# Chunked attention inside an expert block: one visit of TensorE per group, the second head's state in the other half of the partitions, and one load and the stores at other places in their queues

## The chip, the cores and the metric

The kernel runs on one core of a Trainium2 chip. The metric is the device time in microseconds, the median of three runs. TensorE (PE), VectorE (DVE), ScalarE (ACT) and GpSimd (POOL) compute; SyncE (SP) issues all transfers between the chip's memory and the on-chip memory.

## The reference, cut to what matters

```
# B, H, S, D = 4, 8, 768, 48
for t in range(S):
    kt, vt, rt = (k[:, :, t], v[:, :, t], r[:, :, t])
    cur = np.einsum('bhd,bhe->bhde', u[None] * kt, vt)
    y[:, :, t] = np.einsum('bhd,bhde->bhe', rt, state + cur)
    state = w[None, :, :, None] * state + np.einsum('bhd,bhe->bhde', kt, vt)
x = y.transpose(0, 2, 1, 3).reshape(B * S, H * D)          # 3072 x 384
gate = 1.0 / (1.0 + np.exp(-(x @ w_gate)))                 # 384 x 1536
val = x @ w_val
return gate * val @ w_out                                  # 1536 x 384
```

A recurrent attention with a 48 x 48 state per batch and head feeds a gated two-layer block.

## The kernel before, in words

**Attention.** The 768 steps are cut into 12 chunks of 64, and each chunk has two groups of heads, so there are 24 groups (`GROUPS`), numbered n. Per group the kernel computes scores of keys against decayed queries within the chunk (`scores`), keeps their lower triangle (`keep`, VectorE), multiplies them by the values (`apply`), adds what earlier chunks left (`from_state`, queries times state), and makes the state's update (`outer`). These are 16 small float32 matmuls each, 48 or 64 wide, which work in the four 64 x 64 quarters of the array. `decay_state` (ScalarE) scales the state; `add_state` (VectorE) adds the update. The output of a group lies in two PSUM banks (`yb`): `x_high` (ScalarE) rounds it into the block's input, `x_low` (VectorE) keeps the rest, and `fills` moves a few rows by transfers.

**What a group needs.** `load_channels` fetches `chan`, `load_tokens` fetches `toks` and, from group 8 on, `dec<-in_rt`. `queries` (GpSimd) writes `dec` from `chan`, `keys` (VectorE) changes `chan`, `own_tokens` (GpSimd) multiplies `dec`'s second half in two steps, `token_keys` (GpSimd) changes `toks`, and `diagonal` (VectorE) reduces what `own_tokens` made and writes the scores' diagonal. `prepare(n)` is these five.

**The block.** Tokens come in 6 tiles of 512 columns (two chunks), and each tile has 12 slices f of 128 hidden channels; an item is one tile and slice. `up` is 18 matmuls into two banks, `sigmoid` (ScalarE), `product` (VectorE), `h_high` (ScalarE) and `h_low` (GpSimd) make the hidden values in two parts, and `down` is 9 matmuls into three accumulators `acc`. `down` of an item runs behind the next item's `up`. It takes its passes in this order: six matmuls on `h_high`, three on `h_low`. After a tile's last slice, `store` copies each accumulator out, half by ScalarE and half by VectorE, through `wf` tiles of which there are two, and issues the transfer.

**PSUM.** Eight banks: two for the scores (`sc`), three for the accumulators, and a ring of three that `up`'s two banks and a group's two output banks take in turn.

**Order.** Every engine works through its own list in the order in which the program was written; nothing reorders it. The opening is written out step by step in the table `START` (groups 0 to 7, tile 0, all weights): a letter names a step and a number its group or item (`Z` scores, `K` keep, `I` apply, `O` outer, `d` decay, `s` add, `h` and `l` the input's two parts, `U`, `g`, `m`, `H`, `q`, `D` the block, `L`, `X` loads, `R`, `k`, `b`, `T`, `i` the five of `prepare`). Then the loop over the items of tiles 1 to 5 runs, and slices 0, 3, 6 and 9 (`SLOTS`) of tiles 1 to 4 each carry one group, 8 to 23. In a slot before, TensorE visits the group twice: `from_state` and `scores` behind `up`, then the previous item's `down`, then `apply` and `outer`. In the opening `apply` runs `from_state` itself and has TensorE drain in between.

Of the kernel before, what the change touches and what calls it, by code (L numbers as in the profile page):

```python
# [10 lines left out]
F32 = mybir.dt.float32  # L11
# [4 lines left out]
ALU = mybir.AluOpType  # L16
# [4 lines left out]
P = 128  # L21
C = 64
# [22 lines left out]
s.0 I.1 k.2 O.1 R.2 F.0 X.3 s.1 h.1 A.3 Z.2 o0.0 W.3 X.4 l.1 L.4 K.2 W.7 T.2 U.0 R.3 g.0 k.3 I.2  # L45
O.2 c.3 W.4 Z.3 j.2 h.2 d.2 l.2 R.4 m.0 s.2 H.0 F.2 K.3 A.4 j.3 U.1 L.5 g.1 X.5 I.3 w.2 h.3 qv.0
d.3 T.4 T.3 w.3 D.0 k.4 O.3 l.3 R.5 s.3 m.1 Z.4 A.5 U.2 o.2 c.4 g.2 K.4 H.1 I.4 d.4 k.5 O.4 h.4
j.4 X.6 qv.1 Z.5 W.6 w.4 m.2 s.4 H.2 D.1 l.4 o.3 U.3 L.6 L.7 c.5 qv.2 D.2 W.11 g.3 K.5 F.4 o.4 A.6
m.3 j.5 H.3 Tv.5 U.4 g.4 R.6 qv.3 w.5 m.4 W.9 ov.5 F.1 I.5 O.5 H.4 D.3 d.5 h.5 k.6 Z.6 s.5 l.5 A.7
U.5 c.6 F.3 q.4 D.4 g.5 k.7 X.7 j.6 F.5 c.7 m.5 H.5 U.6 T.6 j.7 w.7 K.6 q.5 W.10 D.5 o.7 g.6 w.6  # L50
Rv.7 m.6 H.6 q.6 U.7 c.9 g.7 Z.7 ov.6 I.6 O.6 h.6 d.6 j.9 m.7 D.6 W.8 l.6 s.6 c.8 H.7 w.9 U.8 j.8
q.7 D.7 T.7 g.8 w.8 m.8 o.9 H.8 ov.8 q.8 U.9 g.9 D.8 K.7 U.10 c.10 m.9 c.11 H.9 j.10 g.10 I.7 q.9
m.10 O.7 H.10 h.7 l.7 d.7 w.10 D.9 q.10 s.7 ub L.8 X.8 U.11 D.10 g.11 j.11 m.11 o.10 U.12 F.6 H.11
w.11 g.12 ov.11 q.11 R.8 k.8 b.8 T.8 i.8 m.12 H.12 D.11 U.13 qv.12 g.13 m.13 H.13 qv.13 D.12 F.7
"""


# [1 line left out]
def rwkv_then_moe(ctx: ExitStack, tc: tile.TileContext, wd, ub, ch, tk, rt, wt, rk0, vn0, wd0, out):  # L59
# [20 lines left out]
    def one_bank():  # L80
        return ring.tile([P, 512], F32, name="ring")
# [232 lines left out]
    def into_y(n, half, bank, m, cs, lhsT, rhs, stop):  # L314
# [4 lines left out]
            start=first, stop=stop, skip_group_check=True,  # L319
        )  # L320

    def from_state(n):
        c, g = GROUPS[n]
        for p, p2 in PP:
            for s in range(2):
                for be in range(2):
                    row, m = slice(64 * be, 64 * be + D), D if s else 64
                    at = (4 * (2 * g + p) + 2 * s + p2) * D
                    i = (4 * p + 2 * s + p2) * C
                    into_y(  # L330
                        n, s, be, m, slice((2 * p + p2) * C, (2 * p + p2 + 1) * C),
                        state[row, at : at + m], dec[n][row, 0, i : i + C], False,
                    )


# [1 line left out]
    def scores(n):  # L337
        t, r, k = dec[n], chan[n][:, 0], chan[n][:, 1]
        sc = ga[n] = two_banks()
        if n >= FIRST:  # L340
# [12 lines left out]

    def keep(n):
        sc, t = ga.pop(n), score[n % 2]
        for m, at in ((0, 0), (1, 256))[: 2 if n < FIRST else 1]:
            nc.vector.copy_predicated(  # L357
                t.rearrange("q (b m i) -> q b m i", b=2, m=4),
                masks[:, m].bitcast(I32).unsqueeze(1).unsqueeze(1).broadcast_to([P, 2, 4, C]),
                sc[:, :, at : at + 256].rearrange("q b (m i) -> q b m i", m=4),  # L360
            )

    def apply(n):
        c, g = GROUPS[n]
        v, t = toks[n][:, 1], score[n % 2]
        if n < FIRST:
            yb[n] = one_bank(), one_bank()
            if c:
                from_state(n)
                nc.tensor.drain()  # L370
        for p, p2 in PP:
            for s in range(2):
                for gm in range(2):
                    be, row = gm ^ s, slice(64 * gm, 64 * gm + 64)
                    m, at = D if s else 64, (4 * p + 2 * be + p2) * D
                    i = (4 * be + 2 * p + p2) * C
                    into_y(
                        n, s, be, m, slice((2 * p + p2) * C, (2 * p + p2 + 1) * C),
                        v[row, at : at + m], t[row, i : i + C], True,
                    )  # L380
# [10 lines left out]
                        v[row, at : at + D], True,  # L391
                    )

    def states(n):
        g = GROUPS[n][1]
        st = state[0:112, 8 * g * D : 8 * (g + 1) * D]
        return g, st.rearrange("q (p s x) -> q p s x", p=2, s=2)

    def decay_state(n):
        g, st = states(n)  # L400
        for p in range(2):
            for s in range(2):
                nc.scalar.activation(  # L403
                    st[:, p, s], st[:, p, s], AF.Copy,
                    scale=pw[0:112, 4 * g + 2 * p + s, 64:65],
                )

    def add_state(n):
        g, st = states(n)
        for s in range(2):  # L410
            y = yb[n][s][0:112, 256 : 256 + 4 * D].rearrange("q (p x) -> q p x", p=2)
            if GROUPS[n][0]:
                nc.vector.tensor_tensor(st[:, :, s], st[:, :, s], y, ALU.add)  # L413
            else:
# [160 lines left out]
    def idle_matmuls(k):  # L575
# [40 lines left out]
    def load(n):  # L616
        if n < len(GROUPS):
            load_channels(n)
            load_tokens(n)
# [214 lines left out]
```

## Time and profile before

| | us |
|---|---|
| median of 3 runs | 565.53 |
| lowest and highest run | 565.0, 570.23 |
| span of the profiled execution | 564.3 |
| `up` of tile 1's first slice begins | 136.85 |
| first of a slot's matmuls to the next slot's, f = 0 of tile 2 | 22.13 |
| the same, f = 3 of tile 2 | 21.31 |

The span runs from the first to the last instruction of the profiled execution; the run's time also holds the launch and the end around it. The page gives no other time of the profiled execution. Busy time counts an instruction from start to modelled end, so a busy TensorE is not TensorE at its peak.

### The profile page before, as it was taken

The numbers are of one execution on the slowest core, as the hardware profiler recorded it, in microseconds if no ns is written. First come the engines' busy times: TensorE is split into PE (matmuls) and PEld (weight loads), VectorE is DVE, ScalarE is ACT, GpSimd is POOL, SyncE is SP. The second block draws the span as 40 slices with busy tenths as digits, with TensorE's granted clock in tenths as the row PEclk, the third lists the DMA queues.
The fourth block names the chain that finished last, engine by engine and source line by source line (L and its number), as shares of the span: only waits on it lengthen the run. The fifth ranks groups of instructions, "written<-read, shape, count | busy, mean of one in ns | idle before, by whom it ended". The sixth has DMA issues, their size and how long they took to land. (4 is left out here: it accounts for less than half of the span.)

```text
span 564.3 us, 11903 instructions
## 1 busy us (share of the span) xinstructions
PE 526.4 (93%) x5204; PEld 425.6 (75%) x5204; DVE 222.0 (39%) x348; ACT 170.5 (30%) x358; POOL 209.1 (37%) x165
## 2 busy tenths in 40 slices
PE   1595899999999999999999999999999999999995
PEld 1484778877778778778778788788788777888884
DVE  7798799964422322413313413313313311100101
ACT  4466446541322221322222322222312221212121
POOL 3534233843442533424424324524414411221121
PEclk9999799999999999999999999999999999999999
DMA  8699711030500203410203320113230001100001
GB/s 328 262 358 372 303 31 23 2 101 1 200 19 2 91 1 100 157 62 1 61 32 100 116 95 9 40 51 100 80 125 15 8 5 20 57 0 2 0 1 59
DMA packets 15721, 47.83 MB, mean 85 GB/s; under 512 B 2384, under 2 KB 5200, under 8 KB 14256
## 3 DMA queue, kind: packets, MB, share of 16 engines
q1 hardware_dynamic: 15664, 47.01, 23.7%
q8 instruction: 43, 0.70, 0.5%
q14 instruction: 14, 0.11, 0.1%
HBM read 39.92 MB, written 4.72 MB: 79 GB/s over the span
## 5 line engine op out<-in xcount | busy, mean ns | idle before, releaser
L477 PE MATMUL ring<-xt,wx 128*128 128x512 f32 (+1 forms) x1332 | 320.0, 393 | 4.0 <-DVE state L413 2.6
L477 PEld LDWEIGHTS ring<-xt,wx 128*128 128x128 f32 x1332 | 246.8, 191 | 61.1 <-PE ring L477 4.2
L499 POOL TENSOR_TENSOR h<-sg,h 128x512 fp32r<-128x512 f32 x68 | 93.0, 1367 | 309.9 <-ACT h L495 309.9
L515 PE MATMUL acc<-h,wx 128*128 128x512 f32 (+1 forms) x666 | 164.5, 391 | 1.0 <-DVE h L499 0.7
L490 DVE TENSOR_TENSOR sg<-ring,sg 128x512 f32<-128x512 f32 (+1 forms) x74 | 50.0, 676 | 255.1 <-PE ring L477 251.7
L515 PEld LDWEIGHTS acc<-h,wx 128*128 128x128 f32 x666 | 122.2, 190 | 28.3 <-DVE h L499 0.9
L486 ACT ACTIVATE sg<-ring 128x512 f32<-128x512 f32 (+1 forms) x74 | 43.4, 586 | 158.8 <-PE ring L477 158.3
L495 ACT CAST h<-sg 128x512 fp32r<-128x512 f32 (+1 forms) x74 | 45.0, 609 | 152.0 <-DVE sg L490 152.0
L278 POOL TENSOR_TENSOR dec<-chan,tabk 128x512 f32<-128x512 f32 x22 | 30.6, 1390 | 11.9 <-DMA chan<-in_ch 11.9
L440 DVE TENSOR_TENSOR xt<-ring,xt 112x256 fp32r<-112x256 f32 (+1 forms) x52 | 19.9, 418 | 38.0 <-ACT xt L436 37.1
L246 POOL TENSOR_TENSOR wx<-wf,wx 128x1152 fp32r<-128x1152 f32 (+1 forms) x9 | 24.9, 2768 | 23.6 <-ACT wx L243 23.6
L349 PE MATMUL sc<-dec,chan 48*64 48x64 f32 x768 | 17.3, 231 | 12.2 <-DVE chan L284 10.2
L436 ACT CAST xt<-ring 112x256 fp32r<-112x256 f32 (+1 forms) x52 | 17.1, 374 | 33.7 <-PE ring L317 32.6
L357 DVE COPY_PREDICATED score<-masks,sc 128x512 f32<-128x512 int32 x32 | 24.0, 749 | 6.1 <-PE sc L349 5.8
L288 POOL TENSOR_TENSOR toks<-toks,tabn 128x384 f32<-128x384 f32 x19 | 26.2, 1380 | 0.0
L317 PEld LDWEIGHTS ring<-score,toks 64*48 64x48 f32 (+1 forms) x768 | 14.1, 133 | 14.3 <-issue 12.1
L349 PEld LDWEIGHTS sc<-dec,chan 48*64 48x64 f32 x768 | 14.8, 145 | 13.2 <-DVE chan L284 9.4
L317 PE MATMUL ring<-score,toks 64*48 64x64 f32 (+1 forms) x768 | 17.5, 230 | 7.5 <-DVE score L357 6.5
L403 ACT ACTIVATE state<-state,pw 112x96 f32<-112x96 f32 x80 | 23.4, 365 | 0.3 <-PE ring L317 0.2
L237 DVE SCALAR_TENSOR_TENSOR wf<-wr,wf 128x1152 int32<-128x1152 int32 (+1 forms) x13 | 22.5, 1734 | 0.5
L284 DVE TENSOR_TENSOR chan<-chan,tabk 128x512 f32<-128x512 f32 x24 | 20.1, 838 | 2.9 <-ACT dec L272 2.9
L317 PEld LDWEIGHTS ring<-dec,state 48*48 48x48 f32 (+1 forms) x704 | 12.2, 127 | 8.8 <-issue 6.3
(56 smaller groups left out, 238.9 us busy)
## 6 DMA issues: line engine op xcount, KB each, us to landing
wr<-in_wt SPq DMA_DIRECT2D x11, 1152.0 KB, 10.3
chan<-in_ch SPq DMA_DIRECT2D x24, 512.0 KB, 4.3
toks<-in_tk SPq DMA_DIRECT2D x24, 400.0 KB, 4.5
out_y<-wf SPq DMA_DIRECT2D x17, 256.0 KB, 2.2
dec<-in_rt SPq DMA_DIRECT2D x16, 192.0 KB, 4.1
xt<-xt SPq DMA_DIRECT2D x30, 64.0 KB, 2.3
wr<-in_wt SPq DMA_DIRECT2D x2, 576.0 KB, 5.4
xt<-xt SPq DMA_DIRECT2D x12, 32.0 KB, 3.1
```

The lines of the kernel that those rows point to most:

```text
L246: eng.tensor_tensor(wlo[f][:, c], w32[f][:, c], whi[f][:, c], ALU.subtract)
L278: eng.tensor_tensor(v4(t[:, 0]), v4(chan[n][:, 0]), bc2(table_of(n)[:, :, ::-1]), ALU.mult)
L288: eng.tensor_tensor(v4(k), v4(k), bc2(tabn[:, 4 * g : 4 * g + 4]), ALU.mult)
L317: nc.tensor.matmul(yb[n][bank][64 * half : 64 * half + m, cs], lhsT, rhs, start=first, stop=stop, skip_group_check=True,)
L349: nc.tensor.matmul(sc[64 * gm : 64 * gm + 64, be, o : o + C], kk[row, cs : cs + C], rr[row, cs : cs + C], start=True, stop=True,)
L357: nc.vector.copy_predicated(t.rearrange("q (b m i) -> q b m i", b=2, m=4), masks[:, m].bitcast(I32).unsqueeze(1).unsqueeze(1).broadcast_to ...
L477: nc.tensor.matmul(o[:, self.cols], w[a][:, g * DM + kt * P : g * DM + (kt + 1) * P], self.x[:, kt, b, self.cols], start=(k == 0), stop=(k ...
L486: nc.scalar.activation(sg[:, c], self.pair[f][0][:, c], AF.Sigmoid)
L490: nc.vector.tensor_tensor(sg[:, c], self.pair.pop(f)[1][:, c], sg[:, c], ALU.mult)
L495: nc.scalar.copy(out=h[:, 0, c], in_=sg[:, c])
L499: eng.tensor_tensor(h[:, 1, c], self.sg.pop(f)[:, c], h[:, 0, c], ALU.subtract)
L515: nc.tensor.matmul(self.acc[d][:, self.cols], w[a][:, 2 * DM + d * P : 2 * DM + (d + 1) * P], h[:, b, self.cols], start=(f == 0 and k == 0 ...
```

## The change

- In the loop TensorE visits a group once: `outputs` (its two banks and `from_state`), `scores` of the group after, `apply`, `outer`, all behind `up` and ahead of the previous item's `down`. `Z.8` and `K.8` and all of group 9's preparation move into `START`; `prepare` works two groups ahead, `load` three.
- The state of the second of two heads (s = 1) lies in the other 64 partitions than before. `turn_queries` makes two ScalarE copies of these heads' queries into the other half, and `add_state` adds in three pieces instead of two. Each output region is then written by one half of the rows in `from_state` and `apply` alike, and the drain is left out.
- The third load of a group, `dec<-in_rt`, becomes `load_own`, which `prepare(n)` issues (`Y` in `START`) instead of `load_tokens`.
- `finish` (with the stores of a finished tile) comes behind `x_high`, `x_low`, `add_state` and `keep` in the order of ScalarE and VectorE.

```
 START = """
...
+j.10 g.10 I.7 q.9 m.10 O.7 H.10 h.7 l.7 d.7 w.10 D.9 q.10 s.7 ub L.8 X.8 Y.8 L.9 X.9 Y.9 U.11 D.10
...
+R.9 t.9 qv.12 k.9 g.13 m.13 H.13 Z.8 K.8 qv.13 b.9 T.9 i.9 D.12 F.7
...
-        if n >= FIRST:
-            nc.sync.dma_start(out=dec_of(n)[:, 1, 0 : 8 * D], in_=rt[c, g])
+    def load_own(n):
+        c, g = GROUPS[n]
+        nc.sync.dma_start(out=dec_of(n)[:, 1, 0 : 8 * D], in_=rt[c, g])
...
+    def turn_queries(n):
+        for lo, to in ((0, 64), (64, 0)):
+            src = dec[n][lo : lo + 64, 0].rearrange("q (p s x) -> q p s x", p=2, s=2)
+            nc.scalar.copy(out=turned(n)[to : to + 64], in_=src[:, :, 1])
...
+    def outputs(n):
+        yb[n] = one_bank(), one_bank()
+        if GROUPS[n][0]:
+            from_state(n)
...
     def from_state(n):
...
-                    row, m = slice(64 * be, 64 * be + D), D if s else 64
+                    lo = 64 * (be ^ s)
+                    row, m = slice(lo, lo + D), D if s else 64
...
     def apply(n):
...
         if n < FIRST:
-            yb[n] = one_bank(), one_bank()
-            if c:
-                from_state(n)
-                nc.tensor.drain()
+            outputs(n)
...
     def add_state(n):
-        g, st = states(n)
-        for s in range(2):
-            y = yb[n][s][0:112, 256 : 256 + 4 * D].rearrange("q (p x) -> q p x", p=2)
+        for s, to, lo, rows in ((0, 0, 0, 112), (1, 0, 64, D), (1, 64, 0, D)):
...
     def prepare(n):
         if n < len(GROUPS):
+            load_own(n)
             queries(n)
+            turn_queries(n)
             keys(n)
...
         m.up(f)
+        attend = f in SLOTS and n < 4 * (ti + 2) and n < len(GROUPS)
+        goes_on = attend and GROUPS[n][0] < NC - 1
+        if attend:
+            outputs(n)
+            if n + 1 < len(GROUPS):
+                scores(n + 1)
+            apply(n)
+            if goes_on:
+                outer(n)
         m.gate(f)
...
+        if goes_on:
+            decay_state(n)
         if attend:
-            scores(n)
-            if GROUPS[n][0] < NC - 1:
-                decay_state(n)
-            keep(n)
+            x_high(n)
+            x_low(n)
+            if goes_on:
+                add_state(n)
+            if n + 1 < len(GROUPS):
+                keep(n + 1)
         finish(i - 1)
         if attend:
-            apply(n)
-            if GROUPS[n][0] < NC - 1:
-                outer(n)
-            x_high(n)
-            x_low(n)
-            if GROUPS[n][0] < NC - 1:
-                add_state(n)
-            prepare(n + 1)
+            prepare(n + 2)
             fills(n)
-            load(n + 2)
+            load(n + 3)
             n += 1
```

TensorE's rows in the slot of f = 0 in tile 1, from the end of `from_state` to the start of `apply`, before (`ring` is a bank of the ring, `sc` the scores):

```order
L317 MATMUL ring<-dec,state 64x64 x2
L317 MATMUL ring<-dec,state 48x64 x2
L349 MATMUL sc<-dec,chan 64x64 x16
L515 MATMUL acc_429<-h,wx 128x512 x3
L515 MATMUL acc_430<-h,wx 128x512 x3
L515 MATMUL acc_431<-h,wx 128x512 x3
L317 MATMUL ring<-score_98,toks 64x64 x2
```

and after:

```order
L330 MATMUL ring<-dec,state 64x64 x2
L330 MATMUL ring<-chan,state 48x64 x2
L366 MATMUL sc<-dec,chan 64x64 x16
L330 MATMUL ring<-score_97,toks 64x64 x2
L330 MATMUL ring<-score_97,toks 48x64 x2
```

The `down` between the two visits has gone from here; it stands behind `outer`.

SyncE's list at the same slot, from the last loads issued ahead of it, before (`out_y` is the store, `in_rt` the third load of a group):

```order
L101 DMA chan<-in_ch 128x1024
L106 DMA toks<-in_tk 128x800
L108 DMA dec<-in_rt 128x384
L529 DMA out_y<-wf 128x512 x3
L101 DMA chan<-in_ch 128x1024
```

and after:

```order
L102 DMA chan<-in_ch 128x1024
L107 DMA toks<-in_tk 128x800
L545 DMA out_y<-wf 128x512 x3
L111 DMA dec<-in_rt 128x384
L102 DMA chan<-in_ch 128x1024
```

The third load of the group that `prepare` works on stood ahead of the three stores and now stands behind them.

VectorE's list in the slot of f = 0 in tile 2, before:

```order
L357 COPY_PREDICATED score_98<-masks,sc 128x512
L528 COPY wf<-acc_1629 128x256
L528 COPY wf<-acc_1630 128x256
L528 COPY wf<-acc_1631 128x256
L440 TENSOR_TENSOR xt<-ring,xt 112x2x128 x2
L413 TENSOR_TENSOR state<-state,ring 112x2x96 x2
L284 TENSOR_TENSOR chan<-chan,tabk 128x512
L299 TENSOR_REDUCE bonus_108<-dec 128x2x2x2
L304 TENSOR_TENSOR score_99<-masks,bonus_108 128x512
L490 TENSOR_TENSOR sg<-ring,sg 128x512 x3
```

and after:

```order
L456 TENSOR_TENSOR xt<-ring,xt 112x2x128 x2
L429 TENSOR_TENSOR state<-state,ring 112x2x96
L429 TENSOR_TENSOR state<-state,ring 48x2x96 x2
L374 COPY_PREDICATED score_98<-masks,sc 128x512
L544 COPY wf<-acc_1675 128x256
L544 COPY wf<-acc_1676 128x256
L544 COPY wf<-acc_1677 128x256
L297 TENSOR_TENSOR chan<-chan,tabk 128x512
L312 TENSOR_REDUCE bonus_106<-dec 128x2x2x2
L317 TENSOR_TENSOR score_97<-masks,bonus_106 128x512
L506 TENSOR_TENSOR sg<-ring,sg 128x512 x3
```

The three copies of the stores stood ahead of `x_low` (`xt<-ring`) and the state's add, and now stand behind them and behind `keep`; the reduction of `diagonal` (`bonus<-dec`) still stands ahead of the next item's `product` (`sg<-ring`).

## Rows read from the trace of the kernel before

**Rows 1.** The profile's page, its first part: busy time of TensorE and its weight loads, share of the span, and instructions, then the other engines.

```profile
PE 526.4 (93%) x5204; PEld 425.6 (75%) x5204; DVE 222.0 (39%) x348; ACT 170.5 (30%) x358; POOL 209.1 (37%) x165
```

**Rows 2.** The wait view of the whole span: who waited for what, us in total, times, the longest.

```profile
PE ring L477 <- DVE state L413: 2.6, 4, 0.8
```

**Rows 3.** Timeline of TensorE, tile 1 and the two undisturbed slots of tile 2 (f = 3 and 6 begin at 249.61 and 270.92). Columns: start us, us to the end of the last of the group, engine, line, operation, out<-in, count, and in brackets the idle time before it and what ended it.

```profile
184.53 0.68 PE L317 MATMUL ring<-dec,state 48*64 48x64 f32 x32
185.02 0.65 PE L349 MATMUL sc<-dec,chan 48*64 48x64 f32 x32
185.60 2.32 PE L515 MATMUL acc<-h,wx 128*128 128x512 f32 x9
187.85 0.68 PE L317 MATMUL ring<-score,toks 64*64 64x64 f32 x32
188.35 0.64 PE L317 MATMUL ring<-toks 64*48 64x48 f32 x32
188.92 4.44 PE L477 MATMUL ring<-xt,wx 128*128 128x512 f32 x18
193.20 2.25 PE L515 MATMUL acc<-h,wx 128*128 128x512 f32 x9
195.29 4.34 PE L477 MATMUL ring<-xt,wx 128*128 128x512 f32 x18
199.46 2.25 PE L515 MATMUL acc<-h,wx 128*128 128x512 f32 x9
...
249.61 0.68 PE L317 MATMUL ring<-dec,state 48*64 48x64 f32 x32
...
270.92 0.68 PE L317 MATMUL ring<-dec,state 48*64 48x64 f32 x32
```

**Rows 4.** Timeline of all engines, same columns: the slot of f = 0 in tile 2, where tile 1's accumulators are stored (SPq is SyncE's queue).

```profile
227.48 0.68 PE L317 MATMUL ring<-dec,state 48*64 48x64 f32 x32
...
228.71 0.76 DVE L357 COPY_PREDICATED score<-masks,sc 128x512 f32<-128x512 int32 x1 [0.36 <-PE sc L349]
228.91 1.17 ACT L403 ACTIVATE state<-state,pw 112x96 f32<-112x96 f32 x4
...
230.82 3.32 SPq L529 DMA_DIRECT2D out_y<-wf  x3
...
231.58 1.02 POOL L294 TENSOR_TENSOR dec<-dec,toks 128x384 f32<-128x384 f32 x1
...
232.67 1.01 POOL L295 TENSOR_TENSOR dec<-dec,utab 128x384 f32<-128x384 f32 x1
232.95 0.37 ACT L527 COPY wf<-acc 128x256 f32<-128x256 f32 x1 [2.34 <-DMA out_y<-wf]
233.21 0.65 ACT L436 CAST xt<-ring 112x256 fp32r<-112x256 f32 x2
233.35 0.42 DVE L528 COPY wf<-acc 128x256 f32<-128x256 f32 x1 [2.23 <-ACT wf L527]
...
233.69 0.75 DVE L440 TENSOR_TENSOR xt<-ring,xt 112x256 fp32r<-112x256 f32 x2
234.19 0.42 SPq L101 DMA_DIRECT2D chan<-in_ch  x1
...
234.35 0.61 DVE L413 TENSOR_TENSOR state<-state,ring 112x192 f32<-112x192 f32 x2
...
234.84 2.33 PE L477 MATMUL ring<-xt,wx 128*128 128x512 f32 x9 [0.61 <-DVE state L413]
...
235.21 0.37 SPq L108 DMA_DIRECT2D dec<-in_rt  x1
235.48 0.54 DVE L299 TENSOR_REDUCE bonus<-dec 128x8 f32<-128x384 f32 x1
...
236.06 0.69 DVE L304 TENSOR_TENSOR score<-masks,bonus 128x512 f32<-128x512 f32 x1
...
237.28 0.69 DVE L490 TENSOR_TENSOR sg<-ring,sg 128x512 f32<-128x512 f32 x1 [0.53 <-PE ring L477]
238.00 0.62 ACT L495 CAST h<-sg 128x512 fp32r<-128x512 f32 x1 [3.08 <-DVE sg L490]
```

**Rows 5.** Timeline of TensorE in the opening.

```profile
58.54 0.71 PE L349 MATMUL sc<-chan,dec 48*64 48x64 f32 x16 [4.45 <-issue]
...
74.23 0.69 PE L349 MATMUL sc<-dec,chan 48*64 48x64 f32 x32 [0.84 <-DVE chan L284]
...
93.23 0.64 PE L317 MATMUL ring<-dec,state 48*64 48x64 f32 x32
94.02 0.68 PE L317 MATMUL ring<-score,toks 64*64 64x64 f32 x32
...
114.04 0.68 PE L317 MATMUL ring<-dec,state 48*64 48x64 f32 x32
114.87 0.68 PE L317 MATMUL ring<-score,toks 64*64 64x64 f32 x32 [0.15 <-issue]
```

**Rows 6.** Timeline of VectorE near the end of the opening.

```profile
131.54 0.55 DVE L299 TENSOR_REDUCE bonus<-dec 128x8 f32<-128x384 f32 x1 [2.00 <-POOL dec L295]
```

**Rows 7.** Transfer view of 163 to 172 us, a stretch in which one load alone is issued: tile, queue, count, KB each, median us from issue to landing.

```profile
dec<-in_rt SPq DMA_DIRECT2D x1, 192.0 KB, 2.7
```

**Rows 8.** View of the tile `dec`, the 16 loads of `dec<-in_rt` on SyncE's queue.

```profile
DMA to landing us min/median/max: 2.4/4.1/5.8
```

More of the change, by code (lines that the diff above doesn't have):

```diff
@@ L44 @@
 K.0 o0.1 I.0 W.2 tt w0.0 c.1 tn j.1 Tv.0 L.2 h.0 R.1 w.1 L.3 c.2 o.1 Tv.1 Z.1 l.0 K.1 A.2 O.0 W.5
[L45 to L54, printed above, removed]
+s.0 I.1 k.2 O.1 R.2 t.2 F.0 X.3 s.1 h.1 A.3 Z.2 o0.0 W.3 X.4 l.1 L.4 K.2 W.7 T.2 U.0 R.3 g.0 k.3
+I.2 t.3 O.2 c.3 W.4 Z.3 j.2 h.2 d.2 l.2 R.4 m.0 s.2 H.0 F.2 K.3 A.4 j.3 U.1 L.5 g.1 X.5 I.3 t.4 w.2
+h.3 qv.0 d.3 T.4 T.3 w.3 D.0 k.4 O.3 l.3 R.5 s.3 m.1 Z.4 A.5 U.2 o.2 c.4 g.2 K.4 H.1 I.4 t.5 d.4
+k.5 O.4 h.4 j.4 X.6 qv.1 Z.5 W.6 w.4 m.2 s.4 H.2 D.1 l.4 o.3 U.3 L.6 L.7 c.5 qv.2 D.2 W.11 g.3 K.5
+F.4 o.4 A.6 m.3 j.5 H.3 Tv.5 U.4 g.4 R.6 qv.3 w.5 m.4 W.9 ov.5 F.1 I.5 t.6 O.5 H.4 D.3 d.5 h.5 k.6
+Z.6 s.5 l.5 A.7 U.5 c.6 F.3 q.4 D.4 g.5 k.7 X.7 j.6 F.5 c.7 m.5 H.5 U.6 T.6 j.7 w.7 K.6 q.5 W.10
+D.5 o.7 g.6 w.6 Rv.7 m.6 H.6 q.6 U.7 c.9 g.7 Z.7 ov.6 I.6 t.7 O.6 h.6 d.6 j.9 m.7 D.6 W.8 l.6 s.6
+c.8 H.7 w.9 U.8 j.8 q.7 D.7 T.7 g.8 w.8 m.8 o.9 H.8 ov.8 q.8 U.9 g.9 D.8 K.7 U.10 c.10 m.9 c.11 H.9
+j.10 g.10 I.7 q.9 m.10 O.7 H.10 h.7 l.7 d.7 w.10 D.9 q.10 s.7 ub L.8 X.8 Y.8 L.9 X.9 Y.9 U.11 D.10
+g.11 j.11 m.11 o.10 U.12 F.6 H.11 w.11 g.12 ov.11 q.11 R.8 t.8 k.8 b.8 T.8 i.8 m.12 H.12 D.11 U.13
+R.9 t.9 qv.12 k.9 g.13 m.13 H.13 Z.8 K.8 qv.13 b.9 T.9 i.9 D.12 F.7
 """
@@ L106, in load_tokens @@
         nc.sync.dma_start(out=toks[n], in_=tk[c, g])
-        if n >= FIRST:
-            nc.sync.dma_start(out=dec_of(n)[:, 1, 0 : 8 * D], in_=rt[c, g])
-    ident = const.tile([P, P], F32, name="ident")
-    causal = const.tile([P, P], F32, name="causal")
+    def load_own(n):
+        c, g = GROUPS[n]
+        nc.sync.dma_start(out=dec_of(n)[:, 1, 0 : 8 * D], in_=rt[c, g])
+    turn0 = const.tile([P, 2, P], F32, name="turn0")
+    ident, causal = turn0[:, 0], turn0[:, 1]
     masks = const.tile([P, 2, C], F32, name="masks")
@@ L249, in rwkv_then_moe, with turned @@
     xt, dec, ga, yb = {}, {}, {}, {}
+    def turned(n):
+        if n < FIRST:
+            return turn0
+        return chan[n][:, 0, 0 : 4 * C].rearrange("q (p x) -> q p x", p=2)
     PP = [(p, p2) for p in range(2) for p2 in range(2)]
@@ L326, in from_state @@
                 for be in range(2):
-                    row, m = slice(64 * be, 64 * be + D), D if s else 64
+                    lo = 64 * (be ^ s)
+                    row, m = slice(lo, lo + D), D if s else 64
                     at = (4 * (2 * g + p) + 2 * s + p2) * D
-                    i = (4 * p + 2 * s + p2) * C
+                    i = (4 * p + p2) * C
+                    q = turned(n)[row, p, p2 * C : p2 * C + C] if s else dec[n][row, 0, i : i + C]
                     into_y(
                         n, s, be, m, slice((2 * p + p2) * C, (2 * p + p2 + 1) * C),
-                        state[row, at : at + m], dec[n][row, 0, i : i + C], False,
+                        state[row, at : at + m], q, False,
                     )
@@ L366, in apply @@
         if n < FIRST:
-            yb[n] = one_bank(), one_bank()
-            if c:
-                from_state(n)
-                nc.tensor.drain()
+            outputs(n)
         for p, p2 in PP:
@@ L392, in outer, with states @@
                     )
-    def states(n):
+    def states(n, rows=slice(0, 112)):
         g = GROUPS[n][1]
-        st = state[0:112, 8 * g * D : 8 * (g + 1) * D]
+        st = state[rows, 8 * g * D : 8 * (g + 1) * D]
         return g, st.rearrange("q (p s x) -> q p s x", p=2, s=2)
@@ L408, in add_state @@
     def add_state(n):
-        g, st = states(n)
-        for s in range(2):
-            y = yb[n][s][0:112, 256 : 256 + 4 * D].rearrange("q (p x) -> q p x", p=2)
+        for s, to, lo, rows in ((0, 0, 0, 112), (1, 0, 64, D), (1, 64, 0, D)):
+            st = states(n, slice(to, to + rows))[1][:, :, s]
+            y = yb[n][s][lo : lo + rows, 256 : 256 + 4 * D].rearrange("q (p x) -> q p x", p=2)
             if GROUPS[n][0]:
-                nc.vector.tensor_tensor(st[:, :, s], st[:, :, s], y, ALU.add)
+                nc.vector.tensor_tensor(st, st, y, ALU.add)
             else:
-                nc.vector.tensor_copy(st[:, :, s], y)
+                nc.vector.tensor_copy(st, y)
     def x_of(n, k):
@@ L582, in rwkv_then_moe @@
         "N": idle_matmuls,
-        "L": load_channels, "X": load_tokens, "W": load_weights, "A": bonus_keys, "R": queries,
+        "L": load_channels, "X": load_tokens, "Y": load_own, "W": load_weights, "A": bonus_keys, "R": queries, "t": turn_queries,
         "k": keys, "T": token_keys, "Z": scores, "K": keep, "I": apply, "O": outer,
@@ L604, in rwkv_then_moe, with load @@
         steps[name](*([int(arg)] if arg else []))
+    def load(n):
+        if n < len(GROUPS):
+            load_channels(n)
+            load_tokens(n)
     def prepare(n):
         if n < len(GROUPS):
+            load_own(n)
             queries(n)
+            turn_queries(n)
             keys(n)
@@ L614, in prepare @@
             diagonal(n)
[L616 to L619, printed above, removed]
     n = FIRST
-    load(n + 1)
+    load(n + 2)
     for i in range(n0, len(items)):
```

2 lines of the change are left out of this document (removed).

## The prediction

> **What bounds the kernel now.** I read the page's first two parts, then the timeline of TensorE, then the wait view, then one attention slot on all engines. TensorE is busy for 93% of the span [rows 1], and once the opening stops waiting (74.23 in [rows 5]) its rows follow each other without a gap: from 137 us on, the only wait of note in the wait view is the 2.6 us in four pieces of [rows 2]. So the end is set by the sum of TensorE's work in order, and a wait anywhere else counts only where it reaches TensorE.
>
> The prices on TensorE come from [rows 3]. From one `down` to the next (193.20 to 199.46) a plain item takes 6.26 us. Three items with one attention slot take 21.31 us (249.61 to 270.92), so attention adds 21.31 - 18.78 = 2.53 us. Its four sets of small matmuls start 0.49 or 0.50 us apart when one set follows another (184.53 to 185.02, 187.85 to 188.35). Four such sets are 1.98 us. The other 0.55 us is what two visits cost beyond their sets, in going from large tiles to small ones and back: 0.275 us a visit.
>
> **The change part by part.** *One visit instead of two.* Before, 16 slots make 32 visits. After, 16 slots make one each, and `Z.8` in the opening makes one of its own, since the scores run one group ahead: 17. The sets stay the same in number. That is 15 x 0.275 = 4.1 us less. From below: if the cost sat in each set and not in the visit, nothing would be saved. I take 4.1.
>
> *The ring wait.* Where a tile ends, the slot of f = 0 now copies the finished accumulators out before `x_high`: ScalarE's third copy waits for the first store to land (232.95), then `x_high` (233.21), `x_low` (233.69) and the state's add (234.35) follow, and TensorE waits 0.61 us for the output bank (234.84) [rows 4]. That cycle lasts 22.13 us (227.48 to 249.61) against 21.31, so 0.82 us, and there are four [rows 2]: 3.3 us. After, `x_high` comes directly behind the decay, whose end is at 1.43 + 1.17 = 2.6 us after the slot's first matmul (228.91 in a slot begun at 227.48). The bank comes free near 4 us, and TensorE wants it at 2.05 + 2.25 + 2.1 = 6.4. The wait is gone. Bounds: 2.6 us, the idle time that the wait view records, and 3.6 us.
>
> *The drains.* From `from_state` to `apply` the opening takes 0.79 us (93.23 to 94.02) and 0.83 us (114.04 to 114.87) [rows 5], where a set without a drain takes 0.49: 0.64 us saved at these two. The drain before 74.23 is covered: there TensorE waits 0.84 us for VectorE's keys, more than such a drain costs. The three earliest are covered by the stop of 4.45 us that ends at 58.54. Without that cover all six would give 2.0 us. I take 0.6.
>
> *The second head's state in the other half.* This costs two ScalarE copies of 64x256 a group, for which the nearest row is the 112x256 cast, and a third VectorE add, 0.3 us by the two that take 0.61 together [rows 4]. In the loop both engines have idle time in every slot. In the opening VectorE's added 0.3 us per group falls before waits of its own. I count nothing, and up to 1.5 us if it reaches TensorE before 75 us. `Y.9`, moved ahead of `F.6` on SyncE's queue, holds that fill until group 7's `from_state` at 114 us; the fill is wanted at 137 us.
>
> *`load_own` moves, and this is the large term.* Before, the third load of a group (`dec<-in_rt`) was issued a slot ahead with the other two. After, `prepare(n + 2)` issues it in the slot that uses it, on SyncE's in-order queue, and in the four slots of f = 0 it stands behind the three stores of `finish`. The third store needs the third copy, which needs the first store to have landed, because the staging tiles are two. Behind `own_tokens`, which waits for that load on GpSimd, stands the `h_low` of the next item; behind `diagonal`, which waits for `own_tokens` on VectorE, stands the next item's product, and ScalarE's `h_high` and TensorE's next `down` wait for that. VectorE standing still for this step is seen once in the opening (131.54, 2.00 us) [rows 6].
>
> In us after the slot's first matmul, with intervals of [rows 4]: `x_high` 2.5, `x_low` 3.0 (233.21 to 233.69), adds 3.65 to 4.5 (0.61 for two, so 0.9 for three), `keep` to 5.25 (0.76), first copy to 5.65, first store at 5.7, third ScalarE copy 2.13 later at 7.8 (230.82 to 232.95), third VectorE copy to 8.65 (0.40 later, 0.42 long), `load_own` at 9.05 (0.42 behind the copy's end, as 234.19). A lone load of this kind landed after 2.7 us [rows 7]: 11.75. `own_tokens` takes 2.1 (231.58 to 232.67, and 1.01): 13.9. `diagonal` takes 0.6 and some 0.85: 15.35. `h_high` begins 0.72 behind the product (237.28 to 238.00) and takes 0.62: 16.7, seen by TensorE near 16.8. TensorE is there at: visit 2.05, `down` 2.25, `up` and `down` 6.26, `up` 4.18, in all 14.75. It waits 2.05 us, four times: 8.2 us. `h_low` follows at 18.1, when TensorE's third pass asks for it, so it adds nothing. In the other twelve slots the same load can be issued near 0.6, behind `from_state`, and `own_tokens` begins at 4.1 in any case (231.58 in the slot begun at 227.48): it costs nothing. Bounds by [rows 8]: a landing of 2.4 us gives 7.0 us in all; the median of 4.1 gives 13.8. The median is that of loads issued behind 912 KB of the same group's other two (234.19 and the rows behind it); here these two come behind it, and only the last store is ahead. So I stay at 2.7.
>
> *The sum.* -4.1 - 3.3 - 0.6 + 8.2 = +0.2 us. The profiled span is 564.3 us, 1.2 below the median of the three runs, 565.53; that 1.2 is launch and end and stays. The forecast is 565.7 us: no change.
>
> **The rivals.** *The late load hides* (the store chain is shorter than I have it, or `diagonal` gets done in time): then 565.5 - 8.0 = 557.5. Against it: `load_own` would have to go out before 7 us, and the third store alone can't. For it: nothing but my adding up of ten intervals.
>
> *The load lands late*, slower than before: chan and toks of the next group (912 KB) are issued within a microsecond behind it and share its transfer engines, with the store ahead. It ends above 571 from a landing of 4.1 us on: 565.7 + 4 x 1.4 = 571.3. For it speaks the spread of 2.4 to 5.8 [rows 8].
>
> *The cost sits in the sets.* One visit then saves nothing: 565.7 + 4.1 = 569.8. Against it speaks that sets within a visit start at the bare 0.49.
>
> *The row halves collide.* After, `from_state` writes one bank from both halves of the rows, where before each half had its own bank. `apply` already does what `from_state` will do, and its set takes 0.50 us (187.85 to 188.35) against 0.49 for `from_state` (184.53 to 185.02) [rows 3]; so the trace shows no price. If the two halves had to take turns, the set would take twice 0.49, and 16 slots and 6 groups of the opening would give 22 x 0.49 = 10.8 us: 576.5. [...]
>
> That the change doesn't do what it says is excluded by the order of its instructions, as far as the one visit and the missing drains go.
>
> **How the numbers follow.** Forecast 0.62, with 562.5 to 568.5 of its own (stall 1.75 to 2.4 each, visits 3 to 4.5, opening -1 to +1). The load hides 0.13, lands late 0.13, sets 0.08, halves 0.04. The range from 560 to 571 takes in the forecast, the sets, about half of the late landing and the near edge of the hidden one, some 0.8. A measurement here tells about 1% from no change, that is 559.9 and 571.2: faster 0.15 (the load hides, and a little of the forecast's tail), slower 0.12 (halves, half of the late landing, and a little of the opening), the same 0.73.
>
> **What would show it.** The cycle from `from_state` to `from_state` is 21.04 instead of 21.31 in a slot that no store precedes; after the slot of f = 0 it is 23.1, with TensorE's `down` waiting some 2 us for ScalarE's `h_high`, four times, and GpSimd waiting about 7 us for `dec<-in_rt` there. No `up` waits for the state's add. From `from_state` to `apply` in the opening it is 0.49. The forecast fails if that cycle of f = 0 is 21.1 (the load hid) or over 24.5 (it landed late), or if the opening, whose stops before 75 us I leave as they are, ends over 1 us earlier or later.

## The result, and the profile after

The changed kernel takes 570.32 us (median, 567.28 to 573.02), the kernel before, timed beside it, 565.84 us (563.27 to 570.88): a ratio of 1.0066, 95% interval 1.0041 to 1.0091. That is 4.5 us slower: inside the range and on the side of "no change", but 4.6 us above the forecast and outside the 562.5 to 568.5 that the prediction gave the forecast itself. The profiled execution took 569.63 us, with a span of 567.8 us against 564.3.

The first view is TensorE's timeline, as in [rows 3]: the starts of `from_state` in the slots of f = 0, 3 and 6 of tile 2, the changed kernel (columns as there).

```profile
227.84 0.27 PE L330 MATMUL ring<-dec,state 48*64 48x64 f32 x2
...
253.21 0.27 PE L330 MATMUL ring<-dec,state 48*64 48x64 f32 x2
...
274.20 0.27 PE L330 MATMUL ring<-dec,state 48*64 48x64 f32 x2
```

The undisturbed cycle takes 274.20 - 253.21 = 20.99 us here and 20.94 further on (21.31 before; 21.04 foreseen). The cycle of f = 0 takes 25.37 us, where 23.1 was foreseen. The four cycles of f = 0 take 23.10, 25.37, 24.69 and 23.02 us: 96.18 in all, against 88.63 before. So two came out as forecast and two did not: they are over the 24.5 us that the prediction took for the sign of a load that lands late. What holds TensorE is in the wait view (who waited for what, us in total, times, longest):

```profile
POOL dec L307 <- DMA dec<-in_rt: 33.1, 7, 8.3
...
DVE bonus L312 <- POOL dec L308: 24.1, 9, 4.7
...
PE acc L531 <- ACT h L511: 7.5, 5, 1.9
```

Read from the top, this is the forecast's chain: GpSimd waits for the late load, VectorE for GpSimd, and TensorE's `down` (L531) for `h_high`. The bank wait of [rows 2] is gone. The same cycle on all engines, which answers to [rows 4]:

```profile
233.58 3.96 SPq L545 DMA_DIRECT2D out_y<-wf  x3
...
236.35 0.37 ACT L543 COPY wf<-acc 128x256 f32<-128x256 f32 x1 [4.46 <-PE ring L493]
...
236.75 0.42 DVE L544 COPY wf<-acc 128x256 f32<-128x256 f32 x1 [2.87 <-ACT wf L543]
...
237.23 1.89 PE L531 MATMUL acc<-h,wx 128*128 128x512 f32 x7 [0.41 <-DVE wf L544]
...
237.64 0.37 SPq L111 DMA_DIRECT2D dec<-in_rt  x1
...
240.25 1.01 POOL L307 TENSOR_TENSOR dec<-dec,toks 128x384 f32<-128x384 f32 x1 [8.27 <-DMA dec<-in_rt]
...
243.80 0.68 DVE L506 TENSOR_TENSOR sg<-ring,sg 128x512 f32<-128x512 f32 x1
244.51 0.62 ACT L511 CAST h<-sg 128x512 fp32r<-128x512 f32 x1 [6.46 <-DVE sg L506]
...
245.18 3.92 PE L531 MATMUL acc<-h,wx 128*128 128x512 f32 x9 [1.86 <-ACT h L511]
...
248.94 4.34 PE L493 MATMUL ring<-xt,wx 128*128 128x512 f32 x18
```

In us after the slot's first matmul (227.84): the first store at 5.74 (5.7 foreseen), the load issued at 9.80 (9.05), GpSimd starting on it at 12.41 (11.75), the product at 15.96 (15.35), `down` at 17.34 (16.8). In this cycle the step that ran late is the first store's landing: the third copy begins 2.77 us after the store's issue (at 236.35) where I took 2.13. (The bracket there names `up`, which ended at that moment; the copy doesn't read its banks, and the store landed 0.1 us before, 2.7 us from its issue at 233.58.) It is the longest of the four cycles: in the other three the third copy begins 2.11 to 2.14 us after the first store's issue and the load goes out at 9.14 to 9.19, nearly as foreseen. What I had not foreseen is in the row of 245.18: the nine matmuls behind the wait take 3.92 us instead of 2.25. The view by stretches shows why (stretch, its length, busy time and count of PE, PEld, DVE, ACT and POOL, then TensorE's granted clock, the share of the transfer engines, GB/s):

```profile
240.00:243.30 3.30, 3.30 (x15) 2.33 (x13) 0.88 (x2) 0.00 (x0) 2.97 (x3) 1.00 0.69 251
243.30:245.18 1.88, 0.02 (x1) 0.00 (x1) 1.18 (x2) 0.67 (x2) 0.03 (x1) 1.00 0.00 0
245.18:247.18 2.00, 2.00 (x5) 1.61 (x6) 0.69 (x1) 1.06 (x2) 1.39 (x2) 0.51 0.00 0
247.18:248.94 1.76, 1.76 (x7) 1.35 (x5) 0.00 (x0) 0.00 (x0) 1.18 (x1) 0.58 0.00 0
248.94:253.20 4.26, 4.26 (x19) 3.20 (x17) 0.00 (x0) 0.60 (x1) 0.00 (x0) 1.00 0.00 0
```

TensorE is busy at 1.00, stands still from 243.30 to 245.18, and resumes at a granted clock of 0.51, which lasts into the last matmuls of that `down` (0.58 over 247.18 to 248.94); I call it the lower level. Of the four stops, those that end at 245.18 and 332.76 (1.86 us each) were followed by it, the second 1.1 us after TensorE had resumed and then into the next `up`; those that end at 158.19 (1.78) and 420.17 (1.73) were not: the granted clock was 1.00 behind both, and their nine matmuls took 2.35 and 2.36 us. The same view around the stop that ends at 332.76:

```profile
332.76:333.90 1.14, 1.14 (x5) 0.98 (x6) 0.66 (x1) 0.45 (x1) 1.11 (x1) 1.00 0.00 0
333.90:337.40 3.50, 3.50 (x10) 2.66 (x9) 0.03 (x1) 0.62 (x1) 1.45 (x2) 0.51 0.02 5
```

### The profile page after: what moved, and what is told of

Same layout as the page of the kernel before. It is cut to its first block, busy times and chain, and to the rows that moved or that the text cites. A ratio compares the mean times of both kernels' runs of the same rounds, so it can differ in the third digit from the quotient of the medians.

```text
span 567.8 us, 11996 instructions
## 1 busy us (share of the span) xinstructions
PE 524.7 (92%) x5204; PEld 426.6 (75%) x5204; DVE 238.2 (42%) x370; ACT 186.2 (33%) x402; POOL 207.1 (36%) x165
## 5 line engine op out<-in xcount | busy, mean ns | idle before, releaser
L531 PE MATMUL acc<-h,wx 128*128 128x512 f32 (+1 forms) x666 | 167.8, 396 | 10.7 <-ACT h L511 7.5
L531 PEld LDWEIGHTS acc<-h,wx 128*128 128x128 f32 x666 | 122.8, 192 | 41.1 <-ACT h L511 9.7
L249 POOL TENSOR_TENSOR wx<-wf,wx 128x1152 fp32r<-128x1152 f32 (+1 forms) x9 | 23.4, 2610 | 24.1 <-ACT wx L246 24.1
L307 POOL TENSOR_TENSOR dec<-dec,toks 128x384 f32<-128x384 f32 x16 | 16.7, 1046 | 33.2 <-DMA dec<-in_rt 33.1
L366 PE MATMUL sc<-dec,chan 48*64 48x64 f32 x768 | 17.4, 232 | 11.5 <-DVE chan L297 9.4
L297 DVE TENSOR_TENSOR chan<-chan,tabk 128x512 f32<-128x512 f32 x24 | 26.5, 1102 | 2.4 <-ACT dec L280 2.4
L301 POOL TENSOR_TENSOR toks<-toks,tabn 128x384 f32<-128x384 f32 x19 | 23.4, 1233 | 0.0
L429 DVE TENSOR_TENSOR state<-state,ring 48x192 f32<-48x192 f32 (+1 forms) x60 | 21.0, 351 | 2.1 <-ACT xt L452 0.9
```

What stands on the lines that cost most here:

```text
L249: eng.tensor_tensor(wlo[f][:, c], w32[f][:, c], whi[f][:, c], ALU.subtract)
L366: nc.tensor.matmul(sc[64 * gm : 64 * gm + 64, be, o : o + C], kk[row, cs : cs + C], rr[row, cs : cs + C], start=True, stop=True,)
L531: nc.tensor.matmul(self.acc[d][:, self.cols], w[a][:, 2 * DM + d * P : 2 * DM + (d + 1) * P], h[:, b, self.cols], start=(f == 0 and k == 0 ...
```

## The experiments

My theory: all of the loss is the third load's place behind the stores, first as a wait and then, through the wait, as TensorE's lower clock; the rest of the change gains what the sum says. The rivals: the stores' later place or the added work holds TensorE; any load behind stores is too late; the slow matmuls have another cause than the stop; the gain per slot isn't the price of a visit.

**The load ahead of the stores.**

```diff
     def prepare(n):
         if n < len(GROUPS):
-            load_own(n)
             queries(n)
...
+            if n + 2 < len(GROUPS):
+                load_own(n + 2)
         finish(i - 1)
```

> The changed kernel with one line moved: the load of dec<-in_rt of the group after next is issued on SyncE's queue ahead of the three stores of a finished tile instead of behind them. Nothing else differs. Theory (the late load): at the four tile boundaries it is issued near 2 to 5 us after the slot's first matmul instead of 9.8, the diagonal and the next h_high are in time, TensorE's down waits nothing (7.2 us in four waits go) and, since TensorE no longer stands still for 1.8 us, its clock does not fall behind the wait (some 3.4 us in two of the four): every cycle of f = 0 takes 21.0 to 21.6 us, and the whole is near 559 us (557 to 561), granted clock .99. Rival (the stores' later place, or the added copies and adds, hold TensorE, whatever the load does): the cycles of f = 0 stay above 22.5 us, and the time is 567 to 570.

Measured: 557.46 us (557.09 to 558.33; before 567.11), ratio 0.9814, interval 0.9755 to 0.9873; clock 0.993. Run again in a later experiment, 558.35 against 566.47: 0.9859 (0.9826 to 0.9891). The cycles of f = 0 take 21.01, 21.34, 21.01 and 21.03 us, the others 20.94, but for 21.24, 20.99 and 20.49 in three (21.63, 21.32 and 20.86 there in the kernel before). The cycle that begins at 225.55, all engines:

```profile
226.30 0.33 SPq L111 DMA_DIRECT2D dec<-in_rt  x1
...
231.30 3.63 SPq L545 DMA_DIRECT2D out_y<-wf  x3
...
235.09 0.55 DVE L312 TENSOR_REDUCE bonus<-dec 128x8 f32<-128x384 f32 x1
...
236.99 0.62 ACT L511 CAST h<-sg 128x512 fp32r<-128x512 f32 x1 [1.54 <-DVE sg L506]
...
240.54 2.22 PE L531 MATMUL acc<-h,wx 128*128 128x512 f32 x9
```

The load goes out 0.75 us into the slot, `h_high` is done at 237.61, and `down` comes 2.9 us later without a wait. One line moved takes 96.18 - 84.39 = 11.8 us out of the four cycles. The stores stand where the change put them, and the added copies and adds are there too, so neither holds TensorE by more than the 0.63 us by which these four cycles exceed 20.94.

**The late load alone, in the kernel before.**

```diff
-        if n >= FIRST:
-            nc.sync.dma_start(out=dec_of(n)[:, 1, 0 : 8 * D], in_=rt[c, g])
+        if n == FIRST:
+            load_own(n)
+
+    def load_own(n):
+        c, g = GROUPS[n]
+        nc.sync.dma_start(out=dec_of(n)[:, 1, 0 : 8 * D], in_=rt[c, g])
...
     def prepare(n):
         if n < len(GROUPS):
+            load_own(n)
             queries(n)
```

> The kernel before with that one part of the change alone: the load of dec<-in_rt goes out in the slot that uses it, behind the stores, instead of a slot ahead. Theory (it is the load behind the stores in their later place): in the kernel before the stores' copies are made before x_high, so the load goes out near 6.7 us after the slot's first matmul, the product ends near 13.6, h_high near 14.3, and TensorE's down comes at 15.8: no wait, 565 to 567 us, not to be told from the kernel before. Rival (a load behind the stores is enough): four waits of 1.8 to 2 us and some of the clock's fall, 573 to 577 us.

Measured: 566.51 us against 567.11, ratio 0.9971 (0.9936 to 1.0007). `down` never waits for `h_high`. The slot that begins at 225.52, and then the one disturbed cycle of this execution (25.04 us, begun at 311.58):

```profile
232.27 0.38 SPq L112 DMA_DIRECT2D dec<-in_rt  x1
...
239.57 0.62 ACT L499 CAST h<-sg 128x512 fp32r<-128x512 f32 x1 [6.60 <-DVE sg L494]
...
241.30 1.08 PE L519 MATMUL acc<-h,wx 128*128 128x512 f32 x4
...
320.31 3.83 PE L481 MATMUL ring<-xt,wx 128*128 128x512 f32 x9 [1.98 <-DVE state L417]
```

Issued 6.75 us into the slot instead of 9.80, the load is in time. So the load's new place costs nothing alone and the stores' new place at most 0.63 us; together they cost 11.8. The last row is the old bank wait, here 1.98 us long because the third copy came 3.5 us after the first store's issue (314.93 to 318.42), and its nine matmuls also take 3.83 us, at a granted clock of 0.50 (321 to 323 us): the lower clock follows a stop of TensorE of another cause too.

**The stores back, the load left late.**

```diff
+        finish(i - 1)
+        if attend:
             x_high(n)
             x_low(n)
...
-        finish(i - 1)
-        if attend:
             prepare(n + 2)
```

> The changed kernel with one other part undone: the stores' copies of a finished tile stand ahead of x_high, x_low, the state's adds and keep again, as in the kernel before; the load stays behind the stores. Theory: the third copy ends near 6.9 us after the slot's first matmul, the load goes out near 7 instead of 9.8, and the waits of down for h_high (7.2 us) and the clock's fall (3.4) go; in their place the output bank comes free late again, near 8 us where TensorE wants it at 6.4, so up waits some 1.5 us four times: near 566 us (563 to 568). Rival (the load's lateness is not what holds TensorE): the waits for h_high stay and those for the bank are added, 575 us or more.

Measured: 565.15 us (562.38 to 566.59; before 567.11), ratio 0.9946 (0.9917 to 0.9975). The slot that begins at 227.76:

```profile
235.01 0.37 SPq L111 DMA_DIRECT2D dec<-in_rt  x1
...
235.61 2.34 PE L493 MATMUL ring<-xt,wx 128*128 128x512 f32 x9 [1.44 <-DVE state L429]
...
242.28 0.62 ACT L511 CAST h<-sg 128x512 fp32r<-128x512 f32 x1 [6.31 <-DVE sg L506]
```

The load goes out at 7.25, `down` doesn't wait, and the wait for the output bank is back at 1.44 us: cycles of 22.61 to 22.67, 1.7 above the undisturbed 20.94. Expected and found agree.

**TensorE kept busy through its wait.**

```diff
+        if f == 2 and ti <= 4:
+            sp = two_banks()
+            for _ in range(7):
+                nc.tensor.matmul(sp[:, 0], whi[f][:, 0:P], xt[ti][:, 0, 0, :], start=True, stop=True)
         finish(i - 1)
```

> The changed kernel with seven matmuls 128x512 added (their result is not used) in the place of TensorE's wait at each of the four tile boundaries, before the down that waits for h_high. They take some 1.7 us each time, so TensorE arrives at the same h_high at the same time, but does not stand still. Theory (behind the wait the granted clock falls to its lower level, and that costs some 3.4 us in two of four boundaries): the nine matmuls of that down take 2.25 us at all four boundaries, the clock behind them is 1.0, the four cycles of f = 0 take 23.0 to 23.4 us each, and the time is 566 to 567.5. Rival (those matmuls are slow for another reason, such as operands or banks that come late): two of the cycles still take 24.5 us or more, and the time is 570 to 571.

Measured: 567.07 us against 567.11, ratio 0.9993 (0.9960 to 1.0026), so 3.3 us less than the changed kernel's 570.32. The two were not timed beside each other; by their ratios to the kernel before (1.0066 and 0.9993) it is 4.1. The cycles of f = 0 take 23.33, 23.57, 23.13 and 23.02 us. The same place as the row of 245.18 above, and its clock:

```profile
243.19 1.80 PE L667 MATMUL sc<-xt,wx 128*128 128x512 f32 x7
245.41 2.35 PE L531 MATMUL acc<-h,wx 128*128 128x512 f32 x9 [0.42 <-ACT h L511]
247.60 4.34 PE L493 MATMUL ring<-xt,wx 128*128 128x512 f32 x18
```

```profile
244.00:246.00 2.00, 1.58 (x8) 0.96 (x7) 0.81 (x3) 1.12 (x2) 0.57 (x1) 1.00 0.00 0
246.00:248.00 2.00, 2.00 (x10) 1.59 (x9) 0.58 (x1) 0.62 (x1) 1.42 (x2) 1.00 0.00 0
```

`down` starts nearly as late as before (17.1 us into its slot) but takes 2.35 us, and the clock stays at 1.00. Seven useless matmuls make the kernel faster, which excludes late operands or banks as the cause of the slow ones. The four cycles shrink by 96.18 - 93.05 = 3.13 us. The rows of the changed kernel give the same sum: start to start, the slow `down` at 245.18 took 3.76 us where 2.18 is the rule (158.19 to 160.37), and at 332.76 `down` and the `up` behind it took 0.77 and 0.78 too long: 3.13. That the two agree to the hundredth is chance: the first cycle, which had no slow matmuls, got 0.23 us longer.

**A staging tile for the third copy,** with the load ahead of the stores.

```diff
         for d in range(3):
-            o = wtmp.tile([P, W3], F32, name="wf")[:, 0:512]
+            if d != 1:
+                wide = wtmp.tile([P, W3], F32, name="wf")
+            o = wide[:, 512 * (d % 2) : 512 * (d % 2) + 512]
```

> The kernel with the load ahead of the stores, and beside it one more edit: the first two pieces of a finished tile are copied into the two halves of one staging tile, so the third copy has a staging tile of its own and no longer waits for the first store to land. Theory: what is left at the four tile boundaries (21.01, 21.34, 21.01 and 21.03 us where the other cycles take 20.94) is the wait of the next tile's first down for that third copy; all four cycles take 20.94, 0.6 us less in all, near 557 us, which the times alone can't tell from 557.5. Rival (the 0.4 us at the second boundary has another cause): those four cycles stay as they are.

Measured: 556.91 us against 567.02, ratio 0.9801 (0.9754 to 0.9847). All four cycles of f = 0 take 20.94 us. So the 0.63 us that was left there was the next tile's first `down` waiting for the third copy; that wait came in with the stores' later place. The two kernels with the load first beat both the kernel before (by some 8 to 10 us) and the changed one (12 to 13); the times don't tell them apart.

**The drains of the opening,** with the load ahead of the stores.

```diff
         if n < FIRST:
             outputs(n)
+            if c:
+                nc.tensor.drain()
```

> The kernel with the load ahead of the stores, with the six drains of the opening put back between from_state and apply. By the prediction they cost 0.64 us: two are paid in full, some 0.32 us each (from_state to apply 0.79 to 0.83 us instead of 0.50), the others stand beside waits that last longer; the first up of tile 1, at 137.07 us without them, begins 0.5 to 0.8 us later. Rival (no cover): all six are paid, 2.0 us later. Rival (no price): it begins within 0.2 us of 137.07, since a stop further on absorbs them.

Measured: 556.4 us in a single execution, and `up` of tile 1 begins at about 135.5 us: 1.5 us earlier, which none of the three had foreseen. So the pair was timed side by side:

> The kernel with the load ahead of the stores once more, unchanged, as the partner of the next one on the same chip: 557 to 558 us by both theories.

> The same kernel with the six drains of the opening, timed beside its partner. Its single look gave 556.4 us, and an opening that ended 1.5 us earlier although from_state to apply takes 0.36 us longer at 91 and 112 us. Theory (a drain's price is real and small, and that look fell on a good opening): 0.3 to 1.0 us more than the partner. Rival (standing still a little in the opening spares a stop further on, so the drains cost nothing or gain): 0.5 to 1.5 us less than the partner.

Measured: without drains 558.35 us (557.71 to 560.11), with them 558.82 us (557.16 to 559.19); six executions each, and the two spreads overlap. `from_state` begins at 92.30 and 113.19 us in the latter, and `apply` follows here:

```profile
93.14 0.68 PE L330 MATMUL ring<-score,toks 64*64 64x64 f32 x32 [0.20 <-issue]
...
114.02 0.68 PE L330 MATMUL ring<-score,toks 64*64 64x64 f32 x32 [0.15 <-issue]
```

That is 0.84 and 0.83 us where the changed kernel has 0.45 and 0.50. The local price is as in [rows 5]. But in the profiled executions with drains the loop's first `from_state` begins at 139.8 and 141.1 us, and in the eight without at 141.35 to 142.2. Whether the price reaches the end stays open.

**Two visits again,** with the load ahead of the stores.

```diff
     def finish(i):
         ti, h, f = items[i]
-        moe_of(items[i]).down(f)
+        if not n0 - 1 <= i < len(items) - 1:
+            moe_of(items[i]).down(f)
...
             if n + 1 < len(GROUPS):
                 scores(n + 1)
+        moe_of(items[i - 1]).down(items[i - 1][2])
+        if attend:
             apply(n)
```

> The kernel with the load ahead of the stores, and on TensorE alone the one visit split in two again: from_state and scores, then the nine matmuls of the down before, then apply and outer. Nothing is added on another engine. Theory (the gain per slot is the price of a visit): the undisturbed cycle goes from 20.94 back to 21.21 to 21.31 us, the sum over sixteen slots is 4.3 to 5.9 us, the time 562 to 563.5. Rival (the gain came from elsewhere, such as the shape of from_state or the scores' place ahead): the cycle stays at 20.94 and the time at 557.5.

Measured: 571.01 us (569.26 to 572.86; before 567.02), ratio 1.0061 (1.0031 to 1.0090), far above what I expected. The undisturbed cycle is what the theory says, 273.13 - 251.81 = 21.32 us:

```profile
239.55 1.89 PE L531 MATMUL acc<-h,wx 128*128 128x512 f32 x7 [1.53 <-DVE wf L544]
...
251.81 0.27 PE L330 MATMUL ring<-dec,state 48*64 48x64 f32 x2
...
273.13 0.27 PE L330 MATMUL ring<-dec,state 48*64 48x64 f32 x2
```

So one visit instead of two is worth 21.31 - 20.94 = 0.37 us a slot, with the same sets of the same shape. What I left out stands in the first row: `apply` behind `down` makes `x_high` and the copies of the stores later by 2 us, the third copy ends later, and the first `down` of the next tile waits 1.5 us for it at each tile boundary. These four cycles take 23.04 to 23.11 us, 7.1 above the undisturbed. With 0.37 for each of fifteen cycles, and less the 0.63 that the kernel with the load first has there, that makes 12.0 of the 13.5 us between the two; the rest comes behind the last slot and is not placed. "Nothing is added on another engine" was true, and the copies' start was moved all the same.

**The staging tile alone,** the load left behind the stores (the diff of the staging tile, applied to the changed kernel).

> The changed kernel, its load still behind the three stores, with the wide staging alone: the third copy doesn't wait for the first store's landing. Theory (the load is late because the third store is): the third copies end near 7 us after the slot's first matmul instead of 9, the load goes out near 7.5 instead of 9.8, and the h_high that down waits for ends about 2.3 us earlier: of the four waits of 1.8 us nothing or at most 0.3 us each is left, no fall of the clock, 557 to 559.5 us. Rival (a load queued behind stores lands late whenever it is issued, since it shares their transfer engines): down still waits 1 us or more at each boundary, 564 us or more.

Measured: 561.21 us (559.94 to 561.5; before 567.02), ratio 0.9874 (0.9825 to 0.9923): between the two. The cycles of f = 0 take 21.39, 21.99, 21.38 and 21.41 us. The second, begun at 226.04:

```profile
231.78 2.05 SPq L547 DMA_DIRECT2D out_y<-wf  x3
...
233.94 0.40 SPq L111 DMA_DIRECT2D dec<-in_rt  x1
...
236.61 1.02 POOL L307 TENSOR_TENSOR dec<-dec,toks 128x384 f32<-128x384 f32 x1 [6.43 <-DMA dec<-in_rt]
...
241.55 2.35 PE L531 MATMUL acc<-h,wx 128*128 128x512 f32 x9 [0.75 <-ACT h L511]
```

This is again the longest of the four cycles. The third copies end at 6.4 us, but the load goes out only at 7.90, since SyncE issues the three stores until 233.83 (2.05 us from 231.78), 1.4 us beyond the copies' end; in the other three it goes out at 7.18 to 7.42, 1.7 to 2.0 us earlier than in the changed kernel. There `down` still waits some 0.3 us by its start, here 0.9, and the four cycles exceed the undisturbed 20.94 by 0.44 to 1.05 us. GpSimd starts on it 2.67 us after its issue, no later than the 2.7 of a load alone [rows 7], although the stores are just ahead: the rival of shared transfer engines falls. Of the 3.75 us to the 557.46 with the load first, the cycles hold 1.8; the rest I can't place, though in the profiled execution 2.0 of it comes behind the last slot, where the issue of the last two stores begins 3.27 us behind `down`'s last wait (549.55 to 552.82) instead of 2.38 (547.66 to 550.04), and the span ends 6.4 us after that instead of 5.3.

## Why the prediction was right, and where its size was off

**The visits**, -4.1: right, and too small. The price is 0.37 us a visit, not 0.275: 15 x 0.37 = -5.5. In the changed kernel one set starts 0.45 to 0.50 us behind another, so I had put the four sets at too much and left too little of the 2.53 us for the visits; that is part of the difference. The trace of the kernel before had a row nearer to the price, which I did not read: the weight loads (PEld) stand still ahead of the first small set of each of a slot's two visits.

```profile
249.60 0.54 PEld L317 LDWEIGHTS ring<-dec,state 48*64 48x64 f32 x32 [0.37 <-issue]
...
252.93 0.54 PEld L317 LDWEIGHTS ring<-score,toks 64*64 64x64 f32 x32 [0.35 <-issue]
```

With one visit a slot has one such row, of 0.37 us.

**The bank wait**, -3.3: gone (before, the four cycles exceeded the undisturbed by 3.4 us). In its place came 0.63 us of waiting for the third copy (with the load first; 0.9 in the changed kernel), which my timeline did not ask about: I followed the late copies to the load and not to the accumulators that they free.

**The drains**, -0.6: seen where they stand, not shown at the end.

**The row halves**: `from_state` into one bank from both halves takes 0.50 us (227.84 to 228.34, the start of `scores`). That rival, which needs twice 0.49, is out.

**The late load**, +8.2: the mechanism with all its links is right, four times, and so nearly is its size. By the rows the waits are 1.78, 1.86, 1.86 and 1.73 us, 7.2 in all; by starts they are longer, since a waiting matmul also loses its overlap with the one before (without a wait, the `up` of 257.40 ends at 261.74 by its row, and the next `down` starts at 261.58): from the start of `up` to that of the `down` that waits it is 6.10 to 6.22 us where 4.19 is the rule, 7.9 us in all, and a `down` behind a stop takes 2.19 us, not 2.06: 8.4. I take the sum by starts. The rival of the load that lands late is out too: GpSimd started on it 2.6 us after its issue. So the two cycles of over 24.5 us are not the sign for which the prediction took them.

**The step that failed** is the price of a stop. I took one of 2.05 us to cost 2.05 us. The granted clock fell behind two of the four, and that cost another 3.13 us: the term is 11.5 and not 8.2. The kernel before shows that such a price exists. Behind its stop of 4.45 us, which ends at 58.54 [rows 5], its granted clock is 0.50:

```profile
58.54:64.30 5.76, 5.76 (x40) 5.64 (x40) 3.18 (x3) 1.07 (x4) 2.93 (x2) 0.50 1.04 434
```

I cited that row and did not look at the clock behind it; its stops of 1.42 and 1.54 us, at 47.20 and 51.38, were not followed by the lower level (1.00 in 47.20 to 49.84 and in 51.38 to 54.09), so a stop of 2 us was open. When the clock falls I can't say, and the length of the stop alone doesn't decide it: 1.86 us was followed by it twice and 1.78 was not, and of the stops in the opening that end near 45 us, one of 2.03 us in the changed kernel was not followed by it, and one of 2.00 us in the kernel with the load first was. The stretches behind these two, in that order:

```profile
45.00:47.00 2.00, 2.00 (x99) 1.87 (x99) 1.17 (x3) 1.98 (x6) 0.83 (x1) 1.00 0.67 266
```

```profile
45.78:49.30 3.52, 3.52 (x99) 3.26 (x99) 1.94 (x5) 3.50 (x10) 1.75 (x2) 0.52 0.70 240
```

That 570.32 still lies between 560 and 571 is in part luck: the upper part of that range stood for the sets and the late landing, neither of which happened, and not for the clock, and the visits' larger gain took back 1.4 us.

The sum again, in profiled executions: visits -5.5, bank -3.4, waits for the third copy 0.6 + 0.3 (the 0.3 in the cycle of 227.84, where that copy came later still than with the load first), late load 8.4 + 3.1, the end of the opening -0.4 (it is 0.4 later, of which 0.85 is the set of scores and the visit that moved into it; the set moved out of the last slot, and counts in neither), last store 0.4. That is 3.5 us, and the spans differ by 3.5. The rest to 4.5 lies outside these two executions.

## What to carry to other kernels

When a transfer is moved in an in-order queue, list what stands ahead of it at the rarest place of the loop as well as the commonest: twelve of sixteen slots here were harmless, and four took the whole gain. Price a stop of TensorE as the stop and the clock behind it (8.4 and 3.1 us here); look at the granted clock behind the stops that the trace already has. And follow a delayed copy to every buffer that it frees, not only to the chain one is thinking of: that was missed here in the prediction (0.6 us) and again in the experiment with two visits (7 us).

## What was not expected of the hardware

A stop of 1.86 us was followed by a granted clock of 0.51, once from the start of the `down` behind it and once from 1.1 us after TensorE had resumed; of two stops of 2.0 us in the opening one was followed by 1.00 and the other by 0.52. And TensorE's own useless work is the cheaper choice there: seven matmuls of 128x512 in the place of each wait took 3 to 4 us off the kernel.
